# GpSimd's skip addition emitted ahead of its four additions of x at the ends of scan blocks, in a state-space scan with a gated feed-forward network

## The chip, the cores and the metric

The kernel runs on one core of one Trainium2 chip. The metric is the device time of one execution in microseconds (us); lower is better. The core has five engines with a queue of instructions each: TensorE (PE, matrix products, with its weight loads shown apart as PEld), VectorE (DVE), ScalarE (ACT), GpSimd (POOL), and SyncE (SP), whose queue here only starts DMA transfers. Every engine works through its own queue in the order in which the program emitted the instructions; engines wait for one another by semaphores.

## The reference

The input u (2048 rows of 512 channels) is layer-normalised to xn. From xn come two branches: a long convolution along the rows with one kernel per channel (S4), computed by FFT, plus a skip term; and a feed-forward network with GELU, whose SiLU gates the convolution.

```python
K = jnp.einsum("dn,dnl,dn->dl", Cc, P, dB).real       # one kernel of 2048 taps per channel
Kf, Uf = rfft(pad(K)), rfft(pad(xn.T))
y = irfft(Uf * Kf)[:L].T + xn * Dskip                 # s
g = silu(gelu(xn @ w1 + b1) @ w2 + b2)
return x + s * g
```

The skip `xn * Dskip` needs no operation on the 2048 rows: Dskip is added to tap 0 of each channel's kernel before the transform. For one block of channels that is one small addition for each half of the kernel's rows, the "skip addition" of this case.

## The kernel before, in words

The program has two parts. The first, up to some 395 us, runs the feed-forward network and generates the kernels K; its order is a table (`ORDER`). It is not touched. The second part is the scan: the 512 channels are four blocks b = 0..3 of 128 channels (`NB = 4`). Each block's work is written in eight slots g, emitted two at a time by `two_slots(b, i)` with i = 0..3 for blocks 0 to 2, and one at a time by `slot(b, g)` for block 3. Nothing reorders it: instructions stand in each engine's queue in the order of the code.

The work of three blocks is interleaved in one call of `two_slots(b, i)`:

- For block b: the second step of the forward transform (`second_dft`, L913 on PE), the spectrum's copy (`spectrum`, L921 on ACT), the product of input and kernel spectra (`product`, L931 on DVE, and `combine`, L939 and L941 on DVE), and the first step back (`back_dft`, L950 on PE, into PSUM tiles `sa`; `back_out`, L961).
- For block b + 1: its first forward step. `first_dft(b + 1, u, h, parts)` (L891 on PE, 8 matmuls for each part) reads half h of the input (u = 0) or of the kernel (u = 1) from a tile `in`; `first_out` (L899, on ACT or DVE) copies the result from PSUM to the tile `X`.
- For block b - 1: the last step. `last_dft` (L990 on PE) writes four PSUM tiles `y`; `last_out` multiplies them by the gate on DVE into `gb` (four instructions, L997) and adds x on GpSimd into `xb` (four instructions, L998); `store` (L1001 on SP) writes `xb` out.

All of this happens in the call i = 2 of blocks 1 and 2, called `end` in the code: those are the two ends of blocks of this case. (Block 3 goes through `slot`, which has no block after it.)

PSUM tiles of `first_dft`, `back_dft` and `last_dft` come from one rotation of four banks (`bank`). A new tile waits until the tile that had the bank four turns before has been read.

The kernel rows of block b + 1 are loaded by SP in two halves (`kernel_load` and `kernel_half`, L874) in the call i = 1 of block b; a one-column DVE write ahead of each (`pace`, L801) sets when. `side_skip(b + 1, (h,))` (L879 on GpSimd) adds Dskip to tap 0 of half h. Half 0 is added at the end of the call i = 1, half 1 at the end of the call i = 2, which stands behind `last_out` in GpSimd's queue. The PE reads half 1 in the call i = 3: behind `first_dft(b + 1, 1, 0, (1,))`, the last piece of half 0, come `first_dft(b + 1, 1, 1, (0,))` and later `(1,)`, 8 matmuls each. The trace counts each of these matmuls twice, so that a piece of 8 is shown as 16 records.

In the words below, K0 is `first_dft(b + 1, 1, 0, (1,))`, the last piece of half 0 (16 records); H0 and H1 are `first_dft(b + 1, 1, 1, (0,))` and `(1,)`, the two pieces of half 1 (16 records each).

## Time and profile before

| | |
|---|---|
| median of 3 timed runs | 540.81 us (540.78, 540.81, 542.62) |
| the profiled execution's own time | 539.87 us |
| span from its first to its last instruction | 538.0 us |
| mean granted TensorE clock | 0.993 |
| busy: DVE, ACT, POOL | 428.2 us, 391.2 us, 258.1 us |
| skip additions (L879) | 8, 223 to 245 ns each |
| additions of x (L998) | 12, 1257 to 1289 ns each |

A row of the timeline gives the start and the length of a group of like instructions, engine, line, operation, written tile <- read tiles, the count, and in brackets how long the engine had been idle before it and what ended that. A row of the windows view gives for one stretch of time each engine's busy time with its number of instructions, then the TensorE clock that was granted (1.00 is full speed), the busy share of the DMA engines and the GB/s that they moved. PE ends are modelled, so a busy PE is not always a PE at its peak.

### The profile page before, as it was taken

Reading aid. Unit: us, or ns where it says so; the run is one execution under the profiler, and the core shown is the slowest. Engines: PE = TensorE matmul, PEld = TensorE weight load, DVE = VectorE, ACT = ScalarE, POOL = GpSimd, SP = SyncE. Lnnn points to the kernel's source line nnn. Section 1 sums busy time; section 2 is a strip of 40 time slices with the busy share of each in tenths; the row PEclk is TensorE's granted clock in tenths of the full one; section 3 lists DMA queues with packets and bytes.
Section 4 is the critical chain, followed back from the end, with each engine's and each line's share of the span. In section 5 each row is a group of like instructions: output and inputs, shape, how many; then the busy total and the mean of one; then the engine's idle time right before and its main releaser. Section 6 shows DMA issues by size and latency. Waiting matters only on the chain. (4 is left out here: it accounts for less than half of the span.)

```text
span 538.0 us, 16528 instructions
## 1 busy us (share of the span) xinstructions
PE 517.1 (96%) x6999; PEld 422.4 (79%) x6999; DVE 428.2 (80%) x728; ACT 391.2 (73%) x556; POOL 258.1 (48%) x384
## 2 busy tenths in 40 slices
PE   8899999999999999999999999999999998998993
PEld 7677778777777777777777777778888996988981
DVE  6998999999998689786875777896366696676896
ACT  3688896999987987896978799798375563653430
POOL 5629376746896576869716464564010003003031
PEclk9999999999999999999999999999999999999998
DMA  8937437843229892344137332952568378242553
GB/s 227 316 107 242 127 130 231 295 135 106 93 80 297 291 266 79 136 138 139 42 127 224 111 69 100 183 139 99 178 218 198 65 238 153 84 160 80 178 184 115
DMA packets 86086, 85.84 MB, mean 160 GB/s; under 512 B 41878, under 2 KB 60698, under 8 KB 84988
## 3 DMA queue, kind: packets, MB, share of 16 engines
q1 hardware_dynamic: 76944, 66.43, 42.1%
q0 software_dynamic: 8768, 17.83, 10.8%
q8 instruction: 55, 0.90, 0.7%
q10 hardware_dynamic: 300, 0.53, 0.3%
q14 instruction: 19, 0.16, 0.1%
HBM read 51.22 MB, written 33.55 MB: 158 GB/s over the span
## 5 line engine op out<-in xcount | busy, mean ns | idle before, releaser
L616 POOL TENSOR_TENSOR mm<-mm,rc 128x32 f32<-128x32 f32 (+4 forms) x150 | 97.4, 649 | 11.8
L287 PE MATMUL z<-w2h,hh 128*128 128x512 f32 x224 | 95.7, 427 | 0.0
L248 PE MATMUL f<-xh,w1h 128*128 128x512 f32 x220 | 91.5, 416 | 0.2 <-DVE hl L274 0.2
L250 PE MATMUL f<-xh,w1l 128*128 128x512 f32 x220 | 87.0, 396 | 2.5 <-DVE w1l L233 1.5
L289 PE MATMUL z<-w2h,hl 128*128 128x512 f32 x224 | 87.7, 391 | 0.3 <-issue 0.2
L288 PE MATMUL z<-w2l,hh 128*128 128x512 f32 x224 | 87.7, 391 | 0.0
L249 PE MATMUL f<-xl,w1h 128*128 128x512 f32 x220 | 86.8, 394 | 0.0
L605 DVE SCALAR_TENSOR_TENSOR ra<-ra,ph 128x512 f32<-128x512 f32 x64 | 43.8, 684 | 20.3 <-ACT ra L599 19.4
L913 PE MATMUL s<-X,mc 64*64 64x128 f32 x1536 | 58.7, 272 | 0.6 <-issue 0.6
L931 DVE TENSOR_TENSOR t<-s,uh 128x512 f32<-128x512 f32 x64 | 40.8, 683 | 18.3 <-ACT uh L921 14.9
L262 ACT ACTIVATE f<-f,b1s 128x512 f32<-128x512 f32 x56 | 37.2, 665 | 20.3 <-PE f L250 19.1
L639 DVE TENSOR_TENSOR e<-mm,ra 128x1024 f32<-128x1024 f32 x32 | 43.1, 1350 | 10.3 <-ACT ra L627 4.4
L250 PEld LDWEIGHTS f<-xh,w1l 128*128 128x128 f32 x220 | 41.3, 188 | 12.0 <-DVE w1l L233 2.0
L289 PEld LDWEIGHTS z<-w2h,hl 128*128 128x128 f32 x224 | 42.0, 188 | 10.1 <-DVE hl L274 0.6
L248 PEld LDWEIGHTS f<-xh,w1h 128*128 128x128 f32 x220 | 41.5, 189 | 10.7 <-issue 1.2
L287 PEld LDWEIGHTS z<-w2h,hh 128*128 128x128 f32 x224 | 42.4, 189 | 9.5 <-issue 0.7
L913 PEld LDWEIGHTS s<-X,mc 64*64 64x64 f32 x1536 | 45.4, 133 | 5.7 <-issue 1.0
L613 POOL COPY mm<-rc 128x32 f32<-128x32 f32 x30 | 14.6, 488 | 71.0 <-DVE e L646 41.1
L288 PEld LDWEIGHTS z<-w2l,hh 128*128 128x128 f32 x224 | 42.2, 189 | 8.2
L249 PEld LDWEIGHTS f<-xl,w1h 128*128 128x128 f32 x220 | 41.3, 188 | 9.1
L921 ACT COPY uh<-s 128x512 f32<-128x512 f32 x32 | 18.8, 587 | 40.4 <-PE s L913 23.2
L274 DVE TENSOR_TENSOR hl<-f,hh 128x512 fp32r<-128x512 f32 x56 | 37.8, 682 | 10.8 <-ACT hh L268 10.8
(184 smaller groups left out, 1127.5 us busy)
## 6 DMA issues: line engine op xcount, KB each, us to landing
x<-in_A_u_dram SPq DMA_DIRECT2D x8, 512.0 KB
xs<-x SPq DMA_DIRECT2D x8, 512.0 KB
xt_h<-xh POOLq DMA_DIRECT2D x4, 1024.0 KB, 6.6
xt_l<-xl POOLq DMA_DIRECT2D x4, 1024.0 KB, 9.3
kgd<-ko SPq DMA_DIRECT2D x16, 256.0 KB
za<-zo SPq DMA_DIRECT2D x4, 1024.0 KB
xh<-xt_h POOLq DMA_DIRECT2D x4, 1024.0 KB, 6.5
xl<-xt_l POOLq DMA_DIRECT2D x4, 1024.0 KB, 8.9
```

The source lines that it names most:

```text
L248: PE.matmul(p, wh[:, k, :], xh[:, k, :], start=(k == 0), stop=False)
L249: PE.matmul(p, wh[:, k, :], xl[:, k, :], start=False, stop=False)
L250: PE.matmul(p, wl[:, k, :], xh[:, k, :], start=False, stop=(k == KD - 1))
L274: V.tensor_sub(hl, hf, hh)
L287: PE.matmul(z, hh[:, s], wh, start=(f0 == 0 and not rows), stop=False)
L288: PE.matmul(z, hh[:, s], wl, start=False, stop=False)
L289: PE.matmul(z, hl[:, s], wh, start=False, stop=(f0 == FA - 1))
L605: V.scalar_tensor_tensor(ra[:, 0, c], ra[:, 1, c], MAGIC, p, op0=ALU.subtract, op1=ALU.subtract)
L616: GP.tensor_mul(mv[:, :, 0:3:2, w:2 * w], mv[:, :, 0:3:2, 0:w], rc[:, 2 + 2 * i:4 + 2 * i, :].rearrange("p j c -> p c j").unsqueeze(3).to_ ...
L639: V.tensor_mul(e1, m1.unsqueeze(1).to_broadcast([P, 2, CH, N1]), ra[:, :, :, :N1])
L913: PE.matmul(p[ka * 64:(ka + 1) * 64, r, o, :, jj], w, xf[b][h, c, :, k, :], start=(c == 0), stop=(c == 1), skip_group_check=True)
L931: V.tensor_mul(t, p[:, i, :, 1].unsqueeze(1).to_broadcast([P, 2, 2, P]), uh)
```

## The change

In the call `end` (i = 2 of blocks 1 and 2) the skip addition of half 1 is emitted right ahead of `last_out`, not at the end of the call behind it. In the call i = 2 of block 0, which has no `last_out`, it stays where it was. No instruction is added or removed, and no tile or buffer changes.

```diff
             loads(b, g + 1, 0)
             combine(b, i, 1)
             combine(b, i, 0)
+            side_skip(b + 1, (1,))
             last_out(b - 1, py)
         else:
...
-        if i in (1, 2):
+        if i == 1 or i == 2 and not end:
             side_skip(b + 1, (i - 1,))
         loads(b, g + 1, 1)
```

GpSimd's queue at the ends of blocks 1 and 2, as a difference (`in_2` and `in_3` are the kernel rows of blocks 2 and 3, `xb_5046` and `xb_6194` the results of blocks 0 and 1; in brackets the semaphores that an instruction waits for, DMAHW for transfers):

```order
 L879 TENSOR_TENSOR in_2_5753<-in_2_5753,dsk 128x16 [waits DMAHW5_49,DMAHW1_49,DMAHW6_49,DVE_49,DMAHW7_49,PE_49,Pool_49]
+L879 TENSOR_TENSOR in_2_5753<-in_2_5753,dsk 128x16 [waits DMAHW1_49,DVE_49]
 L998 TENSOR_TENSOR xb_5046<-gb_5045,xb_5046 128x16x32 [waits DMAHW2_49,DMAHW0_49,DMAHW3_49,DMASW3_49,DMAHW4_49,DMASW2_49,DMAHW5_49,DMASW1_49,DMAHW7_49,DMASW0_49,DVE_49]
 L998 TENSOR_TENSOR xb_5046<-gb_5045,xb_5046 128x16x32 [waits DVE_49] x3
-L879 TENSOR_TENSOR in_2_5753<-in_2_5753,dsk 128x16 [waits DMAHW1_49]
 L879 TENSOR_TENSOR in_3_6336<-in_3_6336,dsk 128x16 [waits DMAHW4_49,DMAHW5_49,DMAHW0_49,DMAHW6_49,DVE_49,DMAHW7_49,PE_49,Pool_49]
-L998 TENSOR_TENSOR xb_6194<-gb_6193,xb_6194 128x16x32 [waits DMAHW4_49,DMAHW3_49,DMAHW5_49,DMAHW2_49,DMAHW6_49,DMAHW1_49,DMAHW7_49,DVE_49,Pool_49]
+L879 TENSOR_TENSOR in_3_6336<-in_3_6336,dsk 128x16 [waits DMAHW3_49,DVE_49]
+L998 TENSOR_TENSOR xb_6194<-gb_6193,xb_6194 128x16x32 [waits DMAHW4_49,DMAHW5_49,DMAHW2_49,DMAHW6_49,DMAHW1_49,DMAHW7_49,DVE_49,Pool_49]
 L998 TENSOR_TENSOR xb_6194<-gb_6193,xb_6194 128x16x32 [waits DVE_49] x3
-L879 TENSOR_TENSOR in_3_6336<-in_3_6336,dsk 128x16 [waits DMAHW3_49]
```

Both skip additions of a block's kernel rows now stand ahead of the four additions of x. The moved one waits for its own load (one DMA semaphore) and for a count of DVE.

PE's queue in the call i = 3 of block 1 is the same before and now; these rows (those that wait, and the next ones after them) are where the skip addition is waited for. The names are the PSUM tiles `s_block_u_h_part_rowgroup` and `sa`:

```order
L891 MATMUL s_2_1_1_0_0_6048<-fc,in_2_5753 128x128 [waits DMAHW1_49,DVE_49,Pool_49]
L891 MATMUL s_2_1_1_0_1_6049<-fc,in_2_5753 128x128 [waits DVE_49]
L891 MATMUL s_2_1_1_1_0_6066<-fc,in_2_5753 128x128 [waits Activation_49]
L891 MATMUL s_2_1_1_1_1_6067<-fc,in_2_5753 128x128 [waits Activation_49]
L950 MATMUL sa_1_0_6080<-tcn,Y_1_5800 128x128 [waits Activation_49]
L950 MATMUL sa_1_1_6081<-tcn,Y_1_5800 128x128 [waits Activation_49]
```

The first of H0 (the first row) waits for GpSimd, that is for the skip addition, and for a bank that DVE frees; H1 and the matmuls into `sa` wait for banks that ACT frees. Nothing of PE, DVE, ACT or SP moves within its queue.

## The prediction

> **What bounds the kernel now.** I read the page's busy times first, then what PE waited for in the second half, then the timeline and the chain at the two ends of blocks, and last the granted clock there.

> ```profile
> PE 517.1 (96%) x6999; PEld 422.4 (79%) x6999; DVE 428.2 (80%) x728; ACT 391.2 (73%) x556; POOL 258.1 (48%) x384
> PE s L891 <- POOL in L879: 3.9, 2, 2.3
> PE y L990 <- DVE T L970: 0.6, 2, 0.4
> PE s L913 <- issue: 0.6, 1, 0.6
> PE sa L950 <- DVE Y L939: 0.3, 1, 0.3
> ```

> PE is busy 96% of the span. The other rows are the largest of what PE waited for from 340 us on: 3.9 us, in two pieces, for the skip addition (L879); the next three are 1.5 us together. So in the scan a microsecond taken from PE's waiting is a microsecond of the end, as long as nothing else is late.

> ```profile
> 448.12 2.48 DVE L997 TENSOR_TENSOR gb<-y,gb 128x512 f32<-128x512 f32 x4
> 448.88 4.96 POOL L998 TENSOR_TENSOR xb<-gb,xb 128x512 f32<-128x512 f32 x4 [8.14 <-DMA raw<-xs]
> 450.60 1.16 PE L891 MATMUL s<-fc,in 64*128 64x128 f32 x16
> 453.80 0.22 POOL L879 TENSOR_TENSOR in<-in,dsk 128x16 f32<-128x16 f32 x1
> 454.08 2.99 PE L891 MATMUL s<-fc,in 64*128 64x128 f32 x32 [2.31 <-POOL in L879]
> 488.13 1.16 PE L891 MATMUL s<-fc,in 64*128 64x128 f32 x16
> 490.62 0.23 POOL L879 TENSOR_TENSOR in<-in,dsk 128x16 f32<-128x16 f32 x1
> 490.91 2.06 PE L891 MATMUL s<-fc,in 64*128 64x128 f32 x32 [1.61 <-POOL in L879]
> ```

> In the first end PE is through K0 at 450.60 + 1.16 = 451.76. H0 needs the skip addition, which is 0.22 us long, but stands behind four additions of x that began at 448.88 and take 4.96. PE stands 2.31 us. In the second end K0 ends at 489.29 and PE stands 1.61. H0's bank is no reason: DVE's four multiplies, which free it, end at 450.60.

> ```profile
> 454.08 2.99 PE s L891 x32
> 457.07 2.48 PE sa L950 x32
> 459.55 3.65 PE s L913 x128
> 490.91 2.06 PE s L891 x32
> ...
> 493.22 2.05 PE sa L950 x30
> 495.27 3.65 PE s L913 x128
> ```

> These are the same steps of the two ends in the chain of waits. Behind its wait the first takes 459.55 - 454.08 = 5.47 us, the second 495.27 - 490.91 = 4.36. The reason is the clock:

> ```profile
> 451.58:454.99 3.41, 1.10 (x20) 0.91 (x18) 1.41 (x3) 1.07 (x2) 2.44 (x3) 1.00 0.28 57
> 454.99:458.40 3.41, 3.41 (x38) 3.41 (x36) 1.29 (x2) 2.15 (x3) 0.00 (x0) 0.50 0.75 279
> 489.12:492.54 3.42, 1.81 (x32) 1.64 (x30) 1.10 (x2) 1.52 (x3) 1.73 (x3) 1.00 0.30 110
> 458.00:459.00 1.00, 1.00 (x18) 1.00 (x18) 0.38 (x1) 0.26 (x1) 0.00 (x0) 0.80 0.00 0
> 533.00:534.00 1.00, 0.00 (x0) 0.00 (x0) 0.93 (x1) 0.00 (x0) 0.38 (x1) 0.75 0.67 248
> ```

> After the first wait PE is granted half its clock for 3.41 us, from 454.99 to 458.40 (the 0.80 in the microsecond from 458 sets that edge). The next drop, at the end, falls at about 533.5 (a mean of 0.75 in the microsecond from 533), which is 23 steps of 3.41 us after 454.99: the clock changes at edges of a grid. In the step of the grid before the first drop PE was busy 1.10 of 3.41 us (32%). In the step that holds the second wait it was busy 1.81 (53%), and the clock stayed at 1.00.

> **The change part by part.** Nothing is added or removed. One addition of 0.22 us is moved ahead of four additions of 4.96 in all, twice.

> *The moved addition.* It now waits for its own load and a count of DVE (its column write ahead of the load, and at worst whatever DVE did before `last_out`, over at 448.12). When has the load landed?

> ```profile
> 440.52 0.23 POOL L879 TENSOR_TENSOR in<-in,dsk 128x16 f32<-128x16 f32 x1 [40.49 <-DMA gb<-gd]
> 436.16 0.33 SPq L874 DMA_DIRECT2D in<-kgd  x1
> 437.49 0.43 SPq L874 DMA_DIRECT2D in<-kgd  x1
> 441.84 7.94 SPq L839 DMA_DIRECT2D raw<-xs  x4
> 437.00:443.00 6.00, 6.00 (x140) 5.59 (x140) 5.89 (x12) 3.36 (x7) 0.23 (x1) 1.00 0.92 306
> 452.00:453.00 1.00, 0.00 (x0) 0.00 (x0) 0.99 (x2) 0.87 (x2) 1.00 (x2) 1.00 0.22 33
> 453.00:454.00 1.00, 0.00 (x0) 0.00 (x0) 0.00 (x0) 0.00 (x0) 1.00 (x2) 1.00 0.00 0
> ```

> Half 1 (512 KB) was issued at 437.49, half 0 at 436.16, used at 440.52, 4.36 us later. The same delay puts half 1 at 441.85. The DMA engines moved 306 GB/s for 6 us, 1836 KB, by 443; half 1 and the three transfers ahead of it are 512 + 256 + 256 + 512 = 1536 KB. The latest possible is when all DMA is over, in the microsecond from 452. I take 441.9 to 443: GpSimd is idle then, and the additions of x still start at 448.88. The addition costs nothing there; its cover is 8.14 us of idle GpSimd. If that is gone it costs PE at most the wait it has now.

> *The two waits.* K0's end is now followed at once by H0: -2.31 and -1.61 = -3.92 us. What is late next is the banks. H1 takes K0's two banks, `sa` takes H0's.

> ```profile
> 451.80 1.07 ACT L899 COPY X<-s 128x512 f32<-128x512 f32 x2 [0.42 <-PE s L891]
> 492.10 1.07 ACT L899 COPY X<-s 128x512 f32<-128x512 f32 x2 [1.70 <-PE s L891]
> 493.22 1.86 PEld L950 LDWEIGHTS sa<-tcn,Y 64*128 64x128 f32 x30 [0.19 <-ACT X L899]
> ```

> First end, at full clock: H0 451.76 to 452.79 (half of 2.06). ACT's copies of K0 end at 452.87, and the hand-over is 493.22 - 493.17 = 0.05, so H1 runs 452.92 to 453.95, 0.13 late. ACT copies H0 from 452.95 (492.10 against H0's end at 491.94 gives 0.16) to 454.02, so `sa` is free at 454.07, and with 2.05 ends at 456.12. Today it ends at 459.55: -3.43. Second end: H0 to 490.32, H1 490.44 to 491.47, ACT's copies of H0 to 491.55, `sa` 491.60 to 493.65 instead of 495.27: -1.62. The new bank waits replace the old one at 493.22, so the two waits are won whole.

> *The slow clock.* Of the 3.43, 2.31 is the wait and 1.11 (5.47 - 4.36) the slow clock. Whether a timed execution has the slow stretch is not shown: the grid need not lie alike in each. A wait of 1.61 us did not trip it and one of 2.31 did, so the point lies between; at the middle, 1.96, the grid has to lie in (3.41 + 2.31 - 2 x 1.96) / 3.41 = 53% of its positions for the drop. Bounds 0 and 1.11; I take half, 0.56. [...]

> *What moves along.* `second_dft`, the products and the loads of the next calls follow PE and DVE's column writes, so they move as one. What stays is the end of the additions of x at 453.84 and the stores behind it. Next to be hit would be the tail loads of the next block, which overwrite `xb`:

> ```profile
> 453.87 1.81 SPq L1001 DMA_DIRECT2D out_dram<-xb  x4
> 463.53 0.33 SPq L979 DMA_DIRECT2D gb<-gd  x1
> 464.04 0.34 SPq L979 DMA_DIRECT2D xb<-in_u_rows_dram  x1
> 473.03 0.32 SPq L874 DMA_DIRECT2D in<-kgd  x1
> 477.81 0.23 POOL L879 TENSOR_TENSOR in<-in,dsk 128x16 f32<-128x16 f32 x1 [23.79 <-DVE X L899]
> 478.55 1.16 PE L891 MATMUL s<-fc,in 64*128 64x128 f32 x16
> ```

> The stores have landed by 458 (the row from 458 moves 0 GB/s); the `xb` load moves from 464.04 to 460.6. That leaves 2.6 us. The tightest transfer later is half 0 in the second end, used at 478.04 where PE wants it at 478.55; it is issued by DVE's order, so it moves along.

> Sum on the profiled execution: -3.43 - 1.62 = -5.05, from 539.87 to 534.8. The timed median is 0.94 above the profiled time; for it I take -3.92 - 0.56 = -4.48: 540.81 - 4.5 = **536.3 us**, between 535.8 (the whole 1.11, so -5.0) and 536.9 (none of it).

> **The rivals.**

> 1. *The clock gives nothing.* If gaps this short don't lower the clock in timed executions, only the waits go: 540.81 - 3.92 = 536.9. For it: the second wait left 1.00. Against it: the first did not. [...]

> 2. *ACT takes the place of GpSimd.* If H1 can start only when ACT has copied H0 as well (454.07 and 491.60 in place of 452.92 and 490.44), each end loses 1.15: 536.3 + 2.3 = 538.6. For it: ACT works without a pause there. Against it: four banks, and PE's row of H1 waits for K0's only.

> 3. *The wait is not the skip's.* H0 also waits for DVE's banks. If these were last, nothing moves: 540.8. Against it: DVE was done 3.48 us before PE went on, the skip addition 0.06.

> 4. *Slower: the load lands late.* The skip addition now holds the additions of x, and PE, until half 1 has landed. If that is one load's delay (4.36 us) after PE wants it, PE stands 4.4 + 0.27 in place of 2.31 and 1.61, +5.4, and the second end gets the slow clock too, +1.1: 547.3. It decides from a landing after 453.80 in the first end and 490.62 in the second. Against it: the DMA engines moved nothing from 453 to 454, and before, the addition ran at 453.80 without waiting.

> **How the numbers follow.** Forecast 0.62; rival 1 0.20; rival 2 0.10; rival 3 0.04; rival 4 0.04. Half a percent is 2.7 us, about what can be told from no change, so faster is below 538.1: the forecast, rival 1, and of rival 2 the part with the full clock term, 0.03: 0.85. Same: 0.07 + 0.04 = 0.11. Slower: 0.04. The range is 535.0 to 538.0: below, the clock row's own loss (half of 3.41, 1.7) in place of 1.11, with 0.2 for scatter; above, rival 1 with 0.5 of new bank waits in each end. Rivals 2 to 4 are left out, 0.18.

> **What would show it.** In the changed profile: two skip additions ahead of each four additions of x, the second between 441 and 444, and near 475; no row "PE s L891 <- POOL in L879" in PE's waits; K0, H0 and H1 as one run of 48 records with at most 0.2 us in it; granted clock 1.00 from 440 to the end of PE's work; `sa` of the first end over at about 456.1; the additions of x at 448.9 as before. The forecast is wrong if PE stands over 0.5 us between K0 and `second_dft`, if the additions of x start later against DVE's multiplies than 0.76 us, or if PE's waits in blocks 2 and 3 grow by what was won.

## The result, and the profile after

| | before | changed |
|---|---|---|
| median of 6 timed runs each | 540.63 us (539.38 to 542.62) | 535.66 us (534.37 to 537.21) |
| the profiled execution's own time | 539.87 us | 536.11 us |
| its span | 538.0 us | 534.2 us |

The ratio is 0.9907, 95% interval 0.9885 to 0.9929: 5.0 us faster, between 3.8 and 6.2.

What PE waited for from 340 us on, in the changed kernel's profile:

```profile
PE s L891 <- issue: 2.1, 1, 2.1
PE s L913 <- issue: 0.8, 1, 0.8
PE y L990 <- DVE T L970: 0.6, 2, 0.4
PE sa L950 <- DVE Y L939: 0.3, 1, 0.3
```

The row for the skip addition, 3.9 us before, is gone. The first row is new, and comes back below: a pause of PE with no releaser.

The timeline of the two ends of blocks in the changed kernel (GpSimd, PE and ACT):

```profile
445.48 0.23 POOL L879 TENSOR_TENSOR in<-in,dsk 128x16 f32<-128x16 f32 x1 [3.18 <-DMA in<-kgd]
450.37 4.97 POOL L998 TENSOR_TENSOR xb<-gb,xb 128x512 f32<-128x512 f32 x4 [4.66 <-DMA raw<-xs]
478.07 0.23 POOL L879 TENSOR_TENSOR in<-in,dsk 128x16 f32<-128x16 f32 x1 [2.45 <-DMA in<-kgd]
483.59 4.98 POOL L998 TENSOR_TENSOR xb<-gb,xb 128x512 f32<-128x512 f32 x4 [5.29 <-DVE gb L997]
452.09 3.36 PE L891 MATMUL s<-fc,in 64*128 64x128 f32 x47
486.14 3.36 PE L891 MATMUL s<-fc,in 64*128 64x128 f32 x47
453.28 2.05 ACT L899 COPY X<-s 128x512 f32<-128x512 f32 x4 [0.43 <-PE s L891]
449.61 2.48 DVE L997 TENSOR_TENSOR gb<-y,gb 128x512 f32<-128x512 f32 x4
```

Both skip additions stand ahead of the additions of x, and at the first end those start 0.76 us after DVE's first multiply (450.37 - 449.61), as before. K0, H0 and H1 are one run of PE without a gap (48 records: the last of them is listed by itself, behind the first of `sa`). PE is busy without a pause around both ends, and its granted clock is 1.00:

```profile
440.00:460.00 20.00, 20.00 (x536) 17.46 (x538) 15.78 (x29) 9.74 (x18) 5.43 (x6) 1.00 0.84 200
480.00:500.00 20.00, 20.00 (x507) 17.54 (x508) 15.85 (x26) 7.81 (x15) 4.98 (x4) 1.00 0.28 94
```

The `second_dft` behind K0, H0, H1 and `sa`, in the chain of waits:

```profile
457.44 3.65 PE s L913 x128
...
491.49 3.65 PE s L913 x128
```

From K0's start to `second_dft` it is now 457.44 - 452.09 = 5.35 us at the first end, and 491.49 - 486.14 = 5.35 at the second. Before it was 459.55 - 450.60 = 8.95 and 495.27 - 488.13 = 7.14. The ends of blocks gave 3.60 + 1.79 = 5.39 us in the profile; the profiled time fell by 3.76. A 2.1 us pause ahead of both ends took back more than the difference. It falls on the same place of the program in both profiles, 23 records into two pieces of `first_dft` in block 0. First the kernel before, then the changed one:

```profile
422.37 0.72 PE L891 MATMUL s<-fc,in 64*128 64x128 f32 x9 [0.15 <-issue]
```

```profile
423.97 0.72 PE L891 MATMUL s<-fc,in 64*128 64x128 f32 x9 [2.06 <-issue]
```

Nothing of the change lies ahead of that place, and a later profile of the same changed kernel (`e11_after_again` below) has no pause there. So these 1.91 us between the two profiles are scatter of executions, and only the timed runs can tell the gain.

### The profile page after: what moved, and what is told of

It is laid out like the page before. It is cut to its first block, busy times and chain, and to the rows that moved or that the text cites. A ratio compares the mean times of both kernels' runs of the same rounds, so it can differ in the third digit from the quotient of the medians.

```text
span 534.2 us, 16530 instructions
## 1 busy us (share of the span) xinstructions
PE 516.3 (97%) x6999; PEld 421.5 (79%) x6999; DVE 429.2 (80%) x728; ACT 390.8 (73%) x556; POOL 257.9 (48%) x384
## 4 chain that ended last, share of the span: by engine, by line
PE 81%; DVE 8%; POOL 3%; ACT 3%; issue 3%; DMA 2%; POOLq 0%; DVEq 0%; ACTq 0%
PE s L913 10%; PE z L287 9%; PE z L289 8%; PE z L288 8%; PE f L248 8%; PE f L250 8%; PE f L249 8%; PE s L891 6%; PE kg L655 5%; PE sa L950 5%; PE ph L591 3%; PE y L990 2%; DMA w1s<-in_B_w_dram 1%; DVE hl L274 1%; PE xT L359 1%
## 5 line engine op out<-in xcount | busy, mean ns | idle before, releaser
L913 PE MATMUL s<-X,mc 64*64 64x128 f32 x1536 | 58.8, 272 | 0.8 <-issue 0.8
L913 PEld LDWEIGHTS s<-X,mc 64*64 64x64 f32 x1536 | 45.4, 133 | 6.0 <-issue 2.1
```

The source lines that it names most:

```text
L913: PE.matmul(p[ka * 64:(ka + 1) * 64, r, o, :, jj], w, xf[b][h, c, :, k, :], start=(c == 0), stop=(c == 1), skip_group_check=True)
```

## The experiments

The theory: each end pays its wait by itself, the first one also a slow stretch of the clock in some executions. Against it: the clock has nothing to do with waits this short; the won time is lost to ACT or met again later; the load of half 1 becomes the wait.

**One end at a time.** The addition is moved at one end only (here that of block 1; in the second run `b == 2` stands in both places):

```diff
+            if b == 1:
+                side_skip(b + 1, (1,))
...
-        if i in (1, 2):
+        if i == 1 or i == 2 and not (end and b == 1):
             side_skip(b + 1, (i - 1,))
```

> Only the end of block 1 has the skip addition ahead of the additions of x. If each wait is paid whole: PE's wait of about 2.3 us at the first end is gone, the one of 1.6 us at the second stays; 2.3 us faster by the wait alone, 3.4 if the slow stretch of the clock behind it is in the timed executions of the kernel before, so 537.2 to 538.3 us (ratio 0.994 to 0.996). If ACT's copies took GpSimd's place, 1.2 us of it would be lost: about 539.5 (0.998). If the first wait was won only to be met again at the second end, PE would stand there some 3.9 us and the time would be unchanged.

> Only the end of block 2 has the skip addition ahead. If each wait is paid whole: 1.6 to 1.8 us faster, about 538.9 us (ratio 0.997), with PE's wait of 2.3 us at the first end as before. With the other half alone it should add up to the whole change (5.0 us, 0.9907): 2.3 to 3.4 and 1.6 to 1.8. The clock behind the first wait should fall to 0.50 in this profile if that wait is enough to trip it, unless an edge of the 3.41 us grid cuts the wait so that no step holds more than about 1.6 us of it; by the rival that the slow stretch was an accident it stays at 1.00.

Measured: first end only 537.32 us against 539.98, ratio 0.9956 (0.9932 to 0.9980), 2.4 us; second end only 537.20 us, ratio 0.9953 (0.9937 to 0.9970), 2.5 us. Together 0.0091, against 0.0093 for the whole change: within their intervals the two gains add up, and neither is met again later. The first, 1.1 to 3.7 us, is about its wait alone, without the clock; the second, 1.6 to 3.4 us, is more than the 1.6 to 1.8 that were expected, though its interval reaches down to them. The profile of the run with the first end alone shows a likely reason for each. It is of an execution of 539.84 us, 2.5 above the median of its runs, and one profile can't say how often this happens:

```profile
453.40 3.03 PE L891 MATMUL s<-fc,in 64*128 64x128 f32 x43 [0.68 <-issue]
489.77 2.54 PE L891 MATMUL s<-fc,in 64*128 64x128 f32 x32 [2.05 <-POOL in L879]
487.77:491.18 3.41, 1.41 (x24) 1.41 (x26) 0.88 (x2) 1.27 (x3) 1.95 (x3) 1.00 0.23 86
491.18:494.59 3.41, 3.41 (x35) 3.41 (x34) 1.29 (x2) 0.86 (x2) 0.00 (x0) 0.50 0.62 226
```

At the first end PE has another pause of its own, 0.68 us inside K0, in place of the wait. At the second, where the old order stands, the wait is 2.05 us, 2.00 of it in one step of the grid, and this time the clock falls to 0.50 in the next step. `second_dft` follows H0's start 5.55 us later there (495.32 - 489.77 in the chain of waits), against 4.36 in the kernel before. In the run with the second end alone, the first end's wait of 2.26 us leaves the clock at full speed:

```profile
454.24 2.06 PE L891 MATMUL s<-fc,in 64*128 64x128 f32 x32 [2.26 <-POOL in L879]
449.88:453.29 3.41, 2.09 (x52) 1.73 (x44) 3.26 (x6) 1.66 (x3) 3.41 (x4) 1.00 0.59 88
453.29:456.70 3.41, 2.46 (x36) 2.27 (x38) 0.38 (x1) 1.27 (x3) 0.89 (x2) 1.00 0.55 205
456.70:460.12 3.42, 3.42 (x88) 3.30 (x92) 2.21 (x4) 1.86 (x3) 0.00 (x0) 1.00 0.27 102
```

These stretches are steps of that execution's grid, counted back from the fall after its last matmul (clock 0.69 in the microsecond from 528, so 528.38). An edge at 453.29 cuts the wait in two; PE is busy 2.09 and 2.46 us of the two steps.

**Longer waits, for the clock.** In the kernel before, multiplications by 1 that leave the values as they are stand between the additions of x and the skip addition, at both ends (four here, one and two in the other runs):

```diff
+        if end:
+            for _ in range(4):
+                GP.tensor_scalar(dsk, dsk, 1.0, 0.0, op0=ALU.mult, op1=ALU.add)
         if i in (1, 2):
             side_skip(b + 1, (i - 1,))
```

> The kernel before with one multiplication by 1 on the small tile of Dskip (about 0.3 us on GpSimd, values unchanged) between the additions of x and the skip addition, at both ends. The waits grow to about 2.6 and 1.9 us. If PE's share of work in one 3.41 us step of the grid decides on the clock, a step with over 2.3 us of waiting gives 0.50 in the next step, one with under 1.63 does not; 1.9 is new. [...]

> As the run before with four such multiplications (about 1.2 us): waits of about 3.5 and 2.8 us, 2.4 us more waiting than the kernel before in all. If PE's share of work in a step decides, the clock falls to 0.50 behind both waits unless an edge cuts them near the middle, and the time is 2.4 to 5 us above the kernel before. [...]

> As the run with one multiplication, with two (about 0.7 us): waits of about 3.0 and 2.3 us if PE has no pause of its own ahead of them. If the share of a 3.41 us step decides, with the point between 1.85 and 1.98 us of standing in one step (from the runs so far), the next step is at 0.50 wherever the edges leave over 1.98 us of the wait in one step, and at 1.00 where they leave under 1.85.

Single times: 538.80, 545.03 and 543.09 us, with one, four and two multiplications; the kernel before alone spreads from 537.2 to 542.7 beside them, so only the profiles are read. The waits at the two ends are 0.69 and 2.38 us with one, 3.09 and 2.75 with two, 3.86 and 3.14 with four. The 0.69 missed its 2.6: PE had paused before, in `second_dft` and in K0. The windows by steps of the grid, first with one multiplication (a wait of 2.38 us, cut at 488.01 into 0.53 and 1.86), then with two (3.09 us at the first end, 2.75 at the second), then with four (3.14 us at the second end):

```profile
488.01:491.42 3.41, 1.55 (x27) 1.56 (x28) 0.40 (x1) 0.94 (x3) 1.72 (x3) 1.00 0.40 147
491.42:494.84 3.42, 3.42 (x66) 3.11 (x66) 1.86 (x3) 1.49 (x4) 0.00 (x0) 1.00 0.46 165
```

```profile
456.83 2.06 PE L891 MATMUL s<-fc,in 64*128 64x128 f32 x32 [3.09 <-POOL in L879]
451.87:455.28 3.41, 1.86 (x46) 1.50 (x36) 3.06 (x6) 1.66 (x3) 3.41 (x4) 1.00 0.57 86
455.28:458.69 3.41, 1.86 (x32) 1.87 (x33) 0.00 (x0) 0.67 (x2) 1.32 (x4) 1.00 0.60 223
458.69:462.11 3.42, 3.42 (x72) 3.11 (x72) 2.17 (x4) 2.47 (x4) 0.00 (x0) 1.00 0.23 87
489.42:492.83 3.41, 1.08 (x16) 0.89 (x16) 2.00 (x4) 1.66 (x3) 3.33 (x5) 1.00 0.00 0
492.83:496.24 3.41, 2.99 (x28) 2.99 (x30) 0.00 (x0) 0.88 (x2) 0.28 (x2) 0.50 0.83 308
```

```profile
489.45:492.87 3.42, 1.26 (x24) 0.97 (x16) 1.87 (x3) 1.66 (x3) 3.25 (x6) 1.00 0.00 0
492.87:496.28 3.41, 2.43 (x22) 2.43 (x24) 0.00 (x0) 0.32 (x1) 0.76 (x3) 0.50 0.83 308
496.28:499.69 3.41, 3.41 (x36) 3.41 (x34) 1.29 (x2) 0.75 (x2) 0.00 (x0) 0.50 0.02 5
```

The same order of things in every one of these steps: the clock of a step went by PE's busy time in the step before. Busy 1.08, 1.10 (the kernel before), 1.26 and 1.41 us of 3.41: the next step at 0.50. Busy 1.55, 1.77 (the changed kernel's pause of 2.06), 1.81 and 1.86: the next step at 1.00. The wait of 3.09 us that an edge cuts in the middle cost no clock (1.00 in the next two steps); the one of 2.05 that lies almost whole in one step did (0.50). A step at 0.50 with 2.43 us of work was followed by another at 0.50, one with 2.99 by full speed. So for these stretches of the scan the point lies between 1.86 and 2.00 us of standing in one step. A step in the first part, shown below, puts it elsewhere.

**The pauses.** Are PE's pauses without a releaser its own instructions, held up behind the loads of the next input, which come in 128-byte pieces? (The page of the kernel before lists 74 DMA packets of the kind `instruction`, 1.06 MB.) The loads of blocks 2 and 3 are replaced by loads of as many bytes in 8 KB runs, in the kernel before and in the changed one. The bytes come from other rows, so these two blocks leave out their right input; a third run has the right rows in 8 KB runs, with stores of 128-byte pieces in the first part instead:

```diff
-        SY.dma_start(t[g * N1:(g + 1) * N1], xs.rearrange("(n m) (b g d) -> b g n m d", n=N1, b=NB, g=G)[b, g])
+        src = xs.rearrange("(n m) (b g d) -> b g n m d", n=N1, b=NB, g=G)[b, g]
+        if b > 1:
+            j = (b - 2) * G + g
+            src = xs[j * P:(j + 1) * P, :].rearrange("(n a) (c d) -> n (a c) d", n=N1, d=DB)
+        SY.dma_start(t[g * N1:(g + 1) * N1], src)
```

> The kernel before, but the input rows of blocks 2 and 3 (1 MB each, 128-byte pieces) are loaded as the same number of bytes in pieces of 8 KB from other rows of the same buffer, so the output of those blocks is not the reference's. If PE's short pauses with no releaser (0.15 to 2.06 us near 422 us, 0.4 to 0.9 us near 447 to 453 us) are PE waiting for its own instructions behind those small packets, they are gone: 0.5 to 2 us faster than the kernel before and less scatter than its 538.0 to 542.1; the two waits for the skip addition stay at 1.6 to 2.4 us each. If the pauses are of another origin, they stay and the time is that of the kernel before.

> The changed kernel with the same long-packet loads (wrong rows for blocks 2 and 3). With no pauses for instructions the whole of both waits is won: 3.9 us below the run before_long by the waits alone, 5.0 with the slow clock in every execution, about 4.5 if in half of them. By the rival that the pauses are of another origin, the difference is the one of the change itself (5.0 us of 540.6, with pauses in both).

> The changed kernel, with the normalised rows of blocks 2 and 3 kept in memory channel group by channel group, so that these loads read 8 KB runs; the stores in the first part write the 128-byte pieces in their place. The same loads as in the long-packet run, now with the right rows: if the pauses come from small packets while PE's instructions are short (128 columns and fewer), this is 0.5 to 2 us below the changed kernel, 533.5 to 535. If the small packets cost the same in the first part, where PE's matmuls are 512 columns wide, the time is that of the changed kernel or a little above.

Measured: with the long pieces, the kernel before takes 539.41 us against 539.88, ratio 0.9994 (0.9975 to 1.0013), and the changed one 535.46, ratio 0.9915 (0.9890 to 0.9939). The packets are not the reason: no time is won, and the kernel before with long pieces still pauses:

```profile
450.80 0.94 PE L895 MATMUL s<-fc,in 64*128 64x128 f32 x12 [0.89 <-issue]
452.89 2.06 PE L895 MATMUL s<-fc,in 64*128 64x128 f32 x32 [1.15 <-POOL in L883]
```

These rows show something else (the lines are four further down in this run). PE paused 0.89 us inside K0 and then waited 1.15 for the skip addition, 2.04 together, no more than the wait of 2.26 or 2.31 without a pause: where the wait stands, a pause in K0 costs nothing. The difference of the two long runs, 3.95 us, fits the waits alone (3.9) and does not tell them from 4.5.

The version with rows kept by channel group, the right rows in long pieces, takes 538.96 us, ratio 0.9981 (0.9962 to 1.0000): some 3 us above the changed kernel (535.66 and 535.88). Its first part shows a wait for the weights of the feed-forward network that the changed kernel doesn't have:

```profile
PE f L249 <- ACT w1h L232: 1.8, 1, 1.8
26.04:29.45 3.41, 1.66 (x7) 1.05 (x6) 1.29 (x4) 1.84 (x4) 0.00 (x0) 1.00 1.02 328
29.45:32.86 3.41, 3.41 (x9) 2.43 (x8) 3.21 (x14) 2.30 (x3) 0.00 (x0) 0.50 0.32 97
```

The wait lies in one step of the grid and the next step is at 0.50, which by an estimate from these rows costs up to half of 3.41 us more: both together, up to 3.5 us, are as large as the difference. A load of these weights is issued at 19.65 us here, behind the split stores in SP's queue, and at 14.81 in the changed kernel. That the stores are the cause was not tested by a run. The same rows bound the clock's point: here a step with 1.66 us of work gave half speed, where 1.55 in the scan had given full speed.

**The load of half 1, later.** In both kernels half 1 is loaded with slot 4 in place of slot 2:

```diff
-                    (2, 1): lambda: kernel_half(b + 1, 1), (3, 0): lambda: tails(b - 1, 3)}
+                    (3, 0): lambda: tails(b - 1, 3)}
...
+        if 0 < b < NB - 1 and (g, late) == (4, 1):
+            kernel_half(b + 1, 1)
```

> The kernel before, with half 1 of the next kernel rows loaded some 8 to 9 us later (with the loads of slot 4, second place, in place of slot 2). The skip addition stands behind the additions of x, over at about 453.8 and 490.6, and the load (5.8 to 6.5 us from issue to use in the changed kernel's profile) lands by then or a little before: time as before, within 0.5 us.

> The changed kernel with the same later load. If the moved addition now waits for its load and holds the additions of x and PE behind it: at the first end the load is behind other transfers and lands at 452 to 453.5, so PE stands 0.5 to 2 us there again and the additions of x start 3 to 4 us later than DVE's first multiply instead of 0.8; at the second end the DMA engines are quiet and it lands in 3 to 4 us, before PE wants it. Time 0.5 to 2 us above the changed kernel. By the rival that the order on GpSimd is all that matters, it is the time of the changed kernel.

> The changed kernel once more, beside the two late ones: 4 to 5.5 us below the kernel before. PE's short pauses with no releaser fall on the same places of its program (23 records into the pieces near 422 us, 4 records into K0 near 452 us) with other lengths, and the clock stays at 1.00 at both ends.

Measured against 540.03 us: the kernel before with the late load 539.63, ratio 1.0010 (0.9988 to 1.0032); the changed one with it 536.29, ratio 0.9941 (0.9916 to 0.9966); the changed one as it is 535.88, ratio 0.9935 (0.9906 to 0.9964). The late load costs nothing that can be measured, though the two intervals leave room for the 0.5 to 2 us that were expected. The timeline of the changed kernel with it, at the first end:

```profile
448.50 2.47 DVE L997 TENSOR_TENSOR gb<-y,gb 128x512 f32<-128x512 f32 x4
451.18 0.23 POOL L879 TENSOR_TENSOR in<-in,dsk 128x16 f32<-128x16 f32 x1 [9.18 <-DMA in<-kgd]
451.65 4.94 POOL L998 TENSOR_TENSOR xb<-gb,xb 128x512 f32<-128x512 f32 x4 [0.24 <-issue]
452.40 3.03 PE L891 MATMUL s<-fc,in 64*128 64x128 f32 x43 [0.92 <-issue]
```

The load holds the skip addition until 451.18, and with it the additions of x, which start 3.15 us after DVE's first multiply (0.76 in the changed kernel): the queueing that was expected is there. The expectation that PE stands was wrong: the addition is over at 451.41, before K0 is, and K0 has a pause of 0.92. The additions of x have room, since what comes next from them is a store. In the changed kernel alone K0 paused too, but the pause near 422 us, which was expected there again, did not come:

```profile
452.49 3.03 PE L891 MATMUL s<-fc,in 64*128 64x128 f32 x43 [0.91 <-issue]
```

## Why the prediction was right, and where it was not

The forecast was 536.3 us, 4.5 us won; measured were 535.66 and 5.0 (3.8 to 6.2). The mechanism, two waits of PE behind the additions of x, is shown. That the number came so near is in part luck: terms that were not in the sum stand against each other (0.34 us more at the two ends, pauses of 0.49 in K0, a slow step at the second end in some executions), and the interval holds the waits alone (3.92) as well as the waits with the whole clock term (5.03). On the profiled execution itself the sum gave 534.8, and the measured 536.11 is off by the pause near 422 us.

- **The two waits** (-3.92): right, by the profile and by the runs with one end each, whose gains add up to the whole.
- **Where the banks would hold PE next**: H1 was to start 0.13 us late, and `sa` with ACT's copies. ACT's four copies ran in one piece, PE's 48 records with no gap, and each end won 0.17 us more than worked out (3.60 and 1.79 against 3.43 and 1.62). With that rival 2, ACT in GpSimd's place, falls.
- **The landing of half 1**: the term "the same delay", 4.36 us from issue to use, was too small. The changed kernel issued it at 438.98 and used it at 445.48, 6.50 us later, and 5.83 at the second end. So the moved addition ran at 445.48 and 478.07, outside "between 441 and 444" and past "near 475". The conclusion held because the cover was large: GpSimd stood idle another 4.66 and 5.29 us before the additions of x. Rival 4 needed a landing about 10 us later (453.80, and the 1.49 us by which K0 starts later in this profile, against 445.48); the late load shows the mechanism without the price.
- **The slow clock**: half of 1.11 us was taken because a middle point of 1.96 us gave 53% of the grid's positions. The point was found between 1.86 and 2.00 in the scan; at 1.93 it is (3.41 + 2.31 - 2 x 1.93) / 3.41 = 55%. So rival 1 holds in some executions and not in others, and the timed runs can't tell the two apart. What was missed is that the second end's wait is 1.61 in one execution and 2.05 in another, and so has a share in the slow clock too. And a pause in K0 splits the first wait. Of the four profiles with the old order and no added work at each end, one shows the slow step at the first end (the kernel before) and one at the second (the first end moved alone). So half for the first end is not confirmed by these few, and the second end's share was left out. The length of a wait alone does not tell: one of 2.05 us had 0.50 behind it (the first end moved alone), one of 3.09 had 1.00 (two multiplications, cut by an edge).
- **"The two waits are won whole"**: not in each execution. PE has pauses of its own in K0, which the old wait covered. In the six profiles with the new order at the first end they are 0, 0.68, 0, 0.41, 0.92 and 0.91 us, 0.49 in the mean. This is a likely reason that the first end alone gave 2.4 us and not 2.3 plus half of 1.11, though its interval, 1.1 to 3.7, holds both.
- **Rival 3**, banks of DVE: PE went on at K0's end, so it was the skip addition.

## What to carry to other kernels

Where a short instruction that feeds the bound engine stands in a strict queue behind long ones that feed only a store, the wait in the profile is a first estimate of the gain (3.92 us here, 5.0 measured, 3.8 to 6.2), once the short one's own inputs are known to land before the bound engine wants it. Look at the granted clock behind each wait of the matrix engine: two waits of like length can differ by more than a microsecond in cost (2.31 us with 0.50 behind it in the kernel before, 2.26 with 1.00 in the run with the second end alone: in PE's timeline `second_dft` starts 5.40 and 4.29 us after H0). And expect the next smaller cause to show: what a wait covered is paid when the wait is gone (here the pauses in K0, 0 to 0.92 us).

## What was not expected of the hardware

PE pauses without a releaser, time and again at the same places of its program, with lengths that change from execution to execution: 23 records into the two pieces near 422 us 0.15 us in the kernel before, 2.06 in one profile of the changed one and none in another, 4 records into K0 from 0 to 0.92. With 8 KB loads in place of the 128-byte pieces the pause in K0 was still 0.89 and no time was won. What the pauses are due to stays open; whether PE waits for its own instructions there was not tested.
